# The spread of inverted sums as a planned step of its own, in a one-core attention and MLP kernel

## The chip, the core and the metric

The kernel runs on one core of a Trainium2 chip. Its engines are PE (matmul), ACT (activations, here above all exponentials), DVE (elementwise work), POOL and SyncE (SP), which here only issues DMAs. Each engine takes its instructions in order. The metric is the device time of one execution in microseconds (us), lower is better. Three runs of the kernel before took 878.48, 880.14 and 881.72 us; the median is 880.14.

## The reference

Softmax attention with 32 heads of 20 columns and an MLP with a mish activation are computed from the same input and blended by a sigmoid gate. Cut to what matters:

```python
x = A_x                                   # 1 x 2048 x 640, bf16
g = sigmoid((x * gate_w).sum(-1, keepdims=True))
qkv = (x @ wqkv) -> q, k, v of 32 heads x 2048 x 20
p = softmax(q @ k^T * 20 ** -0.5)
a = (p @ v, heads side by side) @ wo
h = x @ w1 + b1                           # w1: 640 x 1536
b = (h * tanh(log1p(exp(-|h|)) + max(h, 0))) @ w2
out = g * a + (1 - g) * b
```

## The kernel before

**Attention.** The scores are computed in units: one key tile of 128 rows against one chunk `c` of 512 queries, for one head. A group `(c, g)` is one chunk and four heads, 64 units; there are 32 groups and 2048 units. Three units make a slot of three PSUM banks, so there are 683 slots, and slot `s` is worked on at step `s`. PE writes the scores (`score_mms`, L1055), ACT takes the exponential of the whole slot in one instruction (`emit_e`, L1077) into one of five buffers, and PE multiplies by V (`pv`, L1180). Two slots of scores are in PSUM at a time, so PE writes those of step s + 2 while ACT works on s + 1. Each exponential can leave out its third unit, which DVE then computes with four instructions (`emit_x`, L1094, L1110 twice and L1112). Such an offloaded unit makes ACT's instruction 1024 columns wide instead of 1536. `choose` (L1118) decides at each step, from the reckoned backlog of DVE, whether one is taken. In the kernel before there are 202.

**The sums.** V carries a column of ones, so each group's accumulator (bank `ACC`) holds the sums of the exponentials. When a group is through, `group_done` (L1214) copies the accumulator to `OUNG` (L1258), and SyncE gathers the sums into `RR` (L1261). When the planner reckons these to be there, `invert` (L1264) has DVE take the reciprocal (L1265), has SyncE write it to DRAM (`SUMS`, L1266, 8 KB) and, right behind it, read it back spread over the partitions (`BCT`, L1268, 256 KB). L1268 waits for L1266 to land. `times` (L1225) is the multiplication on DVE (L1226) that waits for the spread. These steps come 31 times; the last group goes another way.

**The MLP and the rest.** Queries, keys, values and the MLP are background tasks: matmuls that PE does between the scores, into one PSUM bank (`FB`), which DVE evicts at the end of each task. `h_task` computes 256 rows by 256 columns of h (L845) and adds the bias on DVE (L855). It takes a block of w1 that `load_w1(n)` (L791, L801) has brought into one of two buffers, n mod 2. There are 48 loads of 320 KB: six blocks for each of eight row chunks. Load n + 2 is emitted when task n has emitted its last matmul, and waits for that matmul, because it overwrites the same buffer. From load `FIRST` = 12 on the buffers lie in other memory (in the trace under the name REG instead of W2R), and loads 12 and 13 wait for the tasks that used that memory before.

**The order.** Everything is written down by a planner that runs when the kernel is built. `Plan.add` appends an instruction to its engine's order and reckons its start and end from given costs: `cost` on the engine, `tail` until the result can be used, and for a DMA on SyncE `bulk`, the time for which it holds the queue. Instructions on an engine are executed in the order of these calls, and `Plan.finish` turns dependences into waits on semaphores. An instruction that waits holds back all that stand behind it on its engine, SyncE's DMA issues among them. The main loop (L1455) goes over the steps.

Work for DVE that need not be done at once waits in lists: `norm` (the work on the sums), `soon` (two lanes of offloaded units), `blend` (mish) and `bg`. `work(until)` (L400) takes from them, always the entry that could begin first, as long as it ends before `until` by the planner's clock. An entry is a cost, a function and a dependence; `safe` (L396) adds a margin to the dependence's reckoned end, 0.6 us for one on SyncE. Before each instruction that DVE must do at a fixed place, the helper `dve` (L390) lets `work` run up to the moment when that instruction could start, plus `SLACK` = 0.3 us, or plus `LATER` = 0.9 us when it evicts the background bank (`now["bank"]`) and the background work is not pressing (`now["rate"]` under 0.6). `fill_up` (L1439) adds matmuls without use where PE would be idle for too long: repeated scores, or products into the background bank (`spin`, L1433, which the trace shows at L1436).

Of the kernel before, what the change touches and what calls it, by code (L numbers as in the profile page):

```python
# [54 lines left out]
WIDE = 0.60  # L55
# [2 lines left out]
LANES = 2  # L58
TAKEN = 3.3
SLACK = 0.3  # L60
LATER = 0.9
FREE = 0.2
RISK = {"pe": 0.1, "act": 0.3, "dve": 0.5, "pool": 1.2, "sp": 0.6}
CHAIN = 3.0
# [151 lines left out]
def bass_gated_mix__softmax_full_mha__dense_activation_mish__prompt_kernel(  # L216
# [19 lines left out]
    def sb(name, shape, dt):  # L236
        return st.enter_context(nc.sbuf_tensor(name, shape, dt))
# [21 lines left out]
    RR = sb("RR", [P, 16], FP32)  # L259
# [12 lines left out]
    SUMS = nc.dram_tensor("SUMS", [HG, CW], FP32, kind="Internal")  # L272
# [31 lines left out]
    def w1b(n):  # L304
        return AREAS[n >= FIRST][0][:, n % 2, :, :]
# [6 lines left out]
    def otn(c, g, fast):  # L312

        return QT[:, g, (c - 2) * CW:(c - 1) * CW] if fast and c >= 2 else OTN[:, c % 2, g, :]
# [18 lines left out]
    def attention(pl, fast):  # L333
# [8 lines left out]
        norm = deque()  # L342
# [47 lines left out]
        def dve(fn, deps=(), cost=0.1, kind="F"):  # L390

            ready = max([pl.now["dve"], *(d.t1 + HOP for d in deps if d is not None)])
            work(ready + (LATER if fast and now["rate"] < BUSY and now["bank"] else SLACK))
            return pl.add("dve", fn, deps, cost=cost, kind=kind)
# [5 lines left out]
        def work(until):  # L400
            while True:
                best = None
                lined = sorted([lane for lane in (*soon, blend) if lane], key=lambda lane: lane[0][3])
                for rank, todo in enumerate((norm, *lined, bg)):
                    if todo:
                        cost, fn, dep = todo[0][:3]
                        op = dep() if dep else None
                        begin = pl.now["dve"]
                        if op:
                            begin = max(begin, op.t1 if op.eng == "dve" and not op.slot else safe(op))  # L410
                        if begin + cost <= until and (best is None or begin < best[0] - 0.01):
                            best = (begin, todo, fn)
                if best is None:
                    return
                best[1].popleft()
                best[2]()

        def flush(done):

            while not done():  # L420
                ready = [lane for lane in soon if lane]
                first = min(ready, key=lambda lane: (lane[0][2]().t1 if lane[0][2] else 0.0, lane[0][3]))
                first.popleft()[1]()
# [32 lines left out]
        if fast:  # L456
# [328 lines left out]
                return Task([mm(f) for f in range(NFT)], w * COL, finish, due,  # L785
                            lambda: [*sq_ops[n], m_one] if len(sq_ops.get(n, ())) == NFT else None)

            w1_load, w1_last = {}, {}
            w2_load = []

            def load_w1(n):  # L791

                k = n % 6
                if n < 2:
                    deps = []
                elif n in (FIRST, FIRST + 1):
                    assert len(sq_ops) >= 4
                    deps = list(wkv_read)
                else:
                    deps = [w1_last[n - 2]]  # L800
                w1_load[n] = pl.add("sp", lambda e: e.dma_start(  # L801
                    w1b(n), B_w1[:, k * HW:(k + 1) * HW].rearrange("(f p) c -> p f c", p=P)),
                    deps, f"w1{n % 2}", cost=0.75, tail=1.7, bulk=1.5)

            def load_w2():
                w2_load.append(pl.add("sp", lambda e: e.dma_start(
                    W2, B_w2.rearrange("(f p) c -> p f c", p=P)),
                    [*(ei_free[(0, b)] for b in range(3)), w1_last[FIRST - 2], w1_last[FIRST - 1], *u_free], "w2", cost=0.6, tail=1.7, bulk=9.0))
# [401 lines left out]
        oung_free, rr_read, bc_read = [None], [None], [None]  # L1210
        spread_last = []
        end_done = []

        def group_done(c, g, step, last):  # L1214


            end = c == NC - 1 and g >= NG - 1

            def reads():
                if fast:  # L1220
                    return [low_last[0]] if c >= 2 else [zeros, *turned, *(k_moved if g >= 6 else ())]
                assert c < 2 or g > 0 or len(otn_read[c % 2]) == 8
                return otn_read[c % 2]

            def times(src, deps):  # L1225
                oung_free[0] = bc_read[0] = otn_done[(c, g)] = pl.add("dve", lambda e: e.tensor_tensor(  # L1226
                    otn(c, g, fast), src, BC, ALU.mult), [*deps, *reads()], cost=WIDE)
                if g == NG - 1:
                    otn_read[c % 2] = []

            if end:
                while norm:
                    norm.popleft()[1]()
                if (c, g) == groups[-1]:
                    flush(lambda: not any(soon))
                for at, w in ([cut[(c, g)]] if fast else [(n * HW, HW) for n in range(2)]):
                    cols = slice(at, at + w)
                    src, bc, rr = PS[:, ACC, cols], BC[:, cols], RR[:, at // 32:(at + w) // 32]
                    cost = w * COL * 2.6 + 0.09
                    if (c, g) != groups[-1]:  # L1240
                        held = OUNG[:, cols]
                        last = acc_free[0] = pl.add(
                            "dve", lambda e, src=src: e.tensor_copy(held, src), [last, oung_free[0]], cost=cost)
                        src = held
                    a = pl.add("dve", lambda e, src=src, bc=bc: e.transpose(bc, src), [last, bc_read[0]], cost=cost)
                    a = pl.add("dve", lambda e, bc=bc, rr=rr, w=w: e.reciprocal(rr, bc[:, 0:w:32]), [a, rr_read[0]], cost=0.15)
                    a = pl.add("dve", lambda e, bc=bc, rr=rr, w=w: e.transpose(
                        bc.rearrange("p (a r) -> p a r", r=32), rr.unsqueeze(2).to_broadcast([P, w // 32, 32])),
                        [a], cost=cost)
                    to = otn(c, NG - 1, fast)[:, cols]  # L1250
                    end_done.append(pl.add("dve", lambda e, src=src, bc=bc, to=to: e.tensor_tensor(
                        to, src, bc, ALU.mult), [a, *reads()], cost=cost))
                oung_free[0] = bc_read[0] = rr_read[0] = otn_done[(c, g)] = end_done[-1]
                return
            while oung_free[0] == "busy":
                norm.popleft()[1]()
            src = OUNG[:, :]
            ev = dve(lambda e: e.tensor_copy(src, PS[:, ACC, :]), [last, oung_free[0]], WIDE)  # L1258
            oung_free[0] = "busy"
            acc_free[0] = ev  # L1260
            got = pl.add("sp", lambda e: e.dma_start(  # L1261
                RR[:, :], OUNG[0:P:32, :].rearrange("j (r a) -> j r a", a=16)), [ev, rr_read[0]], "nr0", cost=0.55, tail=1.4)

            def invert():  # L1264
                r = pl.add("dve", lambda e: e.reciprocal(RR[:, :], RR[:, :]), [got], cost=0.25)  # L1265
                rr_read[0] = pl.add("sp", lambda e: e.dma_start(  # L1266
                    SUMS.ap().rearrange("j (r a) -> (j r) a", a=16), RR[:, :]), [r, *spread_last], "nr1", cost=0.4, tail=1.7)
                spread_last[:] = [pl.add("sp", lambda e: e.dma_start(  # L1268
                    BC, SUMS.ap().unsqueeze(1).to_broadcast([HG, 32, CW])),
                    [rr_read[0], bc_read[0]], "nr2", cost=0.55, tail=4.7)]  # L1270
                spread = list(spread_last)
                norm.append((WIDE, lambda: times(src, spread), lambda: spread[-1]))
            norm.append((0.25, invert, lambda: got))


        if fast:
# [30 lines left out]
            tasks.extend(h_task(hc, k, H_AT + int(H_STEP * (6 * hc + k))) for hc in range(2) for k in range(6))  # L1307
            tasks.sort(key=lambda t: t.due)
            later(H_AT - 90, lambda: (load_w1(0), load_w1(1)))
            rest = []  # L1310

# [308 lines left out]

    fast = Plan("f_")
    flags, outs = attention(fast, True)
    fast.finish(sem)
    full = Plan("g_")
    maxima(full)
    attention(full, False)
    full.finish(sem)

# [48 lines left out]
```

## Time and profile before

| | us |
|---|---|
| median of three runs | 880.14 |
| lowest, highest | 878.48, 881.72 |
| the profiled execution | 881.69 |
| its span, first to last instruction | 879.9 |
| mean granted clock of PE | 0.993 |

The page gives for each engine the time in which it was busy and its share of the span. The chain of waits is followed back from the last instruction: at each step to what released it. A row of waits names who waited for whom, with the total in us, how often, and the longest. In a timeline the columns are start, length, engine, line, operation and output<-input, and in brackets the idle time before it with what ended it; neighbouring instructions of one group are merged, and xN counts them. Rows with the queue's name (SPq) are DMA issues, not transfers. Rows of groups end with busy time, mean ns of one, and idle time before it. Rows that begin A:B are windows: length, then busy time and count of PE, weight loads, DVE, ACT and POOL, then PE's granted clock, the mean busy share of the 16 DMA engines, and GB/s.

### The profile page before, as it was taken

The numbers are of one execution on the slowest core, as the hardware profiler recorded it, in microseconds if no ns is written. First come the engines' busy times: TensorE is split into PE (matmuls) and PEld (weight loads), VectorE is DVE, ScalarE is ACT, GpSimd is POOL, SyncE is SP. The second block draws the span as 40 slices with busy tenths as digits, with TensorE's granted clock in tenths as the row PEclk, the third lists the DMA queues.
The fourth block names the chain that finished last, engine by engine and source line by source line (L and its number), as shares of the span: only waits on it lengthen the run. The fifth ranks groups of instructions, "written<-read, shape, count | busy, mean of one in ns | idle before, by whom it ended". The sixth has DMA issues, their size and how long they took to land.

```text
span 879.9 us, 15312 instructions
## 1 busy us (share of the span) xinstructions
PE 744.8 (85%) x6249; PEld 259.3 (29%) x6291; DVE 818.7 (93%) x1421; ACT 858.4 (98%) x714; POOL 15.4 (2%) x29
## 2 busy tenths in 40 slices
PE   8888888888878888888888888898888788998885
PEld 3232232222322233223223233333333233332222
DVE  5899999999588998999999999999999799999996
ACT  6999999999999999999999999999999799999996
POOL 2000000000000000000000000000000000000000
PEclk9999999999999999999999999999999899999999
DMA  9112110011122110131121121111211212010001
GB/s 215 28 50 60 56 32 13 8 49 37 41 60 63 57 57 28 44 100 37 41 64 42 54 74 31 46 32 40 69 48 43 72 34 71 21 32 18 14 14 35
DMA packets 69870, 42.44 MB, mean 48 GB/s; under 512 B 20472, under 2 KB 65776, under 8 KB 69744
## 3 DMA queue, kind: packets, MB, share of 16 engines
q1 hardware_dynamic: 67424, 40.89, 16.5%
q8 instruction: 52, 0.85, 0.4%
q10 hardware_dynamic: 2256, 0.47, 0.3%
q0 software_dynamic: 112, 0.01, 0.1%
q14 instruction: 26, 0.21, 0.1%
HBM read 33.97 MB, written 5.23 MB: 45 GB/s over the span
## 4 chain that ended last, share of the span: by engine, by line
ACT 95%; PE 2%; DMA 1%; DVE 1%; issue 0%; ACTq 0%
ACT ETS L1077 93%; ACT REG L877 2%; DMA REG<-in_B_w_dram 1%; ACT W2R L877 1%; PE PS L1055 1%; PE PS L490 1%; PE PS L845 0%; DVE HB L936 0%; PE PS L1436 0%; PE PS L649 0%; PE PS L658 0%; PE PS L1180 0%; PE PS L769 0%; PE PS L930 0%; DVE HB L855 0%
## 5 line engine op out<-in xcount | busy, mean ns | idle before, releaser
L1077 ACT ACTIVATE ETS<-PS 128x1536 bf16<-128x1536 f32 (+1 forms) x683 | 837.9, 1479 | 6.2 <-PE PS L1055 6.1
L1055 PE MATMUL PS<-QT,KT 32*128 32x512 bf16 (+1 forms) x2267 | 281.7, 379 | 114.7 <-ACT ETS L1077 102.9
L1180 PE MATMUL PS<-ETS,V_all 128*21 128x512 bf16 (+1 forms) x1901 | 211.5, 380 | 0.3 <-ACT ETS L1077 0.3
L1055 PEld LDWEIGHTS PS<-QT,KT 32*128 32x128 bf16 x2267 | 69.3, 91 | 324.9 <-ACT ETS L1077 302.6
L1180 PEld LDWEIGHTS PS<-ETS,V_all 128*21 128x21 bf16 x1901 | 48.6, 89 | 93.4 <-issue 89.1
L906 PE MATMUL PS<-W2R,HB 128*128 128x320 bf16 x384 | 71.6, 302 | 0.9 <-DVE OUTT L936 0.6
L1110 DVE SCALAR_TENSOR_TENSOR EM<-EM 128x512 f32<-128x512 f32 x101 | 68.9, 682 | 0.1
L1110 DVE SCALAR_TENSOR_TENSOR ER<-ER 128x512 f32<-128x512 f32 x101 | 68.7, 680 | 0.0
L1094 DVE TENSOR_SCALAR XE<-PS 128x512 f32<-128x512 f32 x80 | 54.7, 686 | 8.3 <-PE PS L1055 7.2
L845 PE MATMUL PS<-XB,REG 128*128 128x256 bf16 x360 | 55.2, 279 | 3.7 <-DMA REG<-in_B_w_dram 3.4
L1094 DVE TENSOR_SCALAR REG<-PS 128x512 f32<-128x512 f32 x74 | 50.7, 686 | 2.2 <-PE PS L1055 1.8
L538 PE MATMUL PS<-XB,WOQ 128*128 128x512 bf16 x135 | 42.2, 384 | 2.7 <-issue 2.4
L906 PEld LDWEIGHTS PS<-W2R,HB 128*128 128x128 bf16 x384 | 30.0, 97 | 36.7 <-issue 24.4
L855 DVE TENSOR_TENSOR HB<-PS,B1F 128x512 bf16<-128x512 f32 x48 | 32.9, 685 | 6.0 <-PE PS L845 5.8
L845 PEld LDWEIGHTS PS<-XB,REG 128*128 128x128 bf16 x360 | 29.9, 98 | 28.7 <-issue 22.3
L1094 DVE TENSOR_SCALAR W2R<-PS 128x512 f32<-128x512 f32 x48 | 32.9, 686 | 3.1 <-PE PS L1055 2.4
L896 DVE SCALAR_TENSOR_TENSOR U<-U,HB 128x512 f32<-128x512 f32 x48 | 32.8, 683 | 0.0
L895 DVE SCALAR_TENSOR_TENSOR U<-U 128x512 f32<-128x512 f32 x48 | 32.7, 680 | 0.0
L550 DVE CAST QT<-PS 128x512 bf16<-128x512 f32 x31 | 21.3, 687 | 7.2 <-PE PS L538 6.8
L1110 DVE SCALAR_TENSOR_TENSOR ER<-XE 128x512 f32<-128x512 uint16 x40 | 27.4, 685 | 0.2
L1110 DVE SCALAR_TENSOR_TENSOR EM<-XE 128x512 f32<-128x512 uint16 x40 | 27.3, 683 | 0.2
L1112 DVE SCALAR_TENSOR_TENSOR XE<-ER,XE 128x512 int32<-128x512 f32 x40 | 27.4, 684 | 0.1
(115 smaller groups left out, 797.3 us busy)
## 6 DMA issues: line engine op xcount, KB each, us to landing
REG<-in_B_w_dram SPq DMA_DIRECT2D x36, 320.0 KB, 3.2
BCT<-SUMS SPq DMA_DIRECT2D x31, 256.0 KB
W2R<-in_B_w_dram SPq DMA_DIRECT2D x12, 320.0 KB, 3.2
KT<-KS SPq DMA_DIRECT2D x28, 128.0 KB
KS<-OTN SPq DMA_DIRECT2D x16, 128.0 KB, 1.8
W2R<-in_B_w_dram SPq DMA_DIRECT2D x1, 1920.0 KB, 9.4
out_dram<-OUTT SPq DMA_DIRECT2D x24, 80.0 KB, 1.6
REG<-in_A_wqkv_dram SPq DMA_DIRECT2D x2, 700.0 KB, 8.2
```

Of the source, the lines that this page charges most:

```text
L538: return lambda e, bank: e.matmul(PS[:, bank, :], pads[:, b, f, :], xt(c)[:, f, :], start=(f == 0), stop=(f == NFT - 1))
L845: return lambda e, bank: e.matmul(PS[:, bank, i * HW:(i + 1) * HW], w1b(n1)[:, f, i * P:(i + 1) * P], xt(c)[:, f, cols], start=(f == 0), s ...
L855: ev = dve(lambda e: e.tensor_tensor(hb, PS[:, bank, :].rearrange("p (i t) -> p i t", i=2), bias, ALU.add), [last, *b1f, *sq_read.values() ...
L895: piece(WIDE, lambda e: e.scalar_tensor_tensor(U2[:, :], U2[:, :], EVEN[0], U2[:, :], ALU.add, ALU.mult))
L896: piece(WIDE, lambda e, to=to: e.scalar_tensor_tensor(U2[:, :], U2[:, :], EVEN[1], to, ALU.add, ALU.mult))
L906: return lambda e, bank: e.matmul(PS[:, bank, 0:HALF], HB[:, hc % 2, f, t * P:(t + 1) * P], W2[:, f, half * HALF:(half + 1) * HALF], start ...
L1055: op = pl.add("pe", lambda e, i=i, g=real(g), tile=tile, j=j, cols=cols, c=c, of_q=of_q: e.matmul(scores(s)[:, i, cols], KT[32 * j:32 * j ...
L1077: e_op[s] = pl.add("act", lambda e: e.activation(ETS[:, s % NETS, 0:n, :], scores(s)[:, 0:n, :], AF.Exp, scale=SCALE, bias=LIFT if fast el ...
L1094: ev_op[s] = dve(lambda e: e.tensor_scalar(y, scores(s)[:, 2, :], SCALE * ULPS, BIAS, ALU.mult, ALU.add), [s_op[s], ei_free[b], *(wkv_read ...
L1110: piece(WIDE, lambda e, v=m if i else f, i=i: e.scalar_tensor_tensor(m, v, STEPS[i], v, ALU.add, ALU.mult), lambda i=i: () if i else [lane ...
L1112: piece(WIDE, lambda e: e.scalar_tensor_tensor(x, m, LAST_STEP, y, ALU.mult, ALU.add))
L1180: lasts[n] = pl.add("pe", lambda e, tile=tile, h=real(g) * HG + j, j=j, src=src[:, cols], of_q=of_q, count=count: e.matmul(PS[32 * j:32 * ...
```

## The change

`invert` no longer issues the spread. It puts an entry `spread` into `norm`, at no cost, whose dependence is the write of the inverted sums; the spread is emitted when `work` takes that entry, and only then does the multiplication enter the list. The reckoned tail of the write grows from 1.7 to 2.8 us. Each load of w1 also depends on the last load emitted for the same of the two buffers. `LATER` becomes 0.5. The number of offloaded units becomes 204, as a result of the planner's reckoning.

```diff
-LATER = 0.9
+LATER = 0.5
...
-            w1_load, w1_last = {}, {}
+            w1_load, w1_last, w1_newest = {}, {}, {}
...
                     deps = [w1_last[n - 2]]
+                deps = [*deps, w1_newest.get(n % 2)]
                 w1_load[n] = pl.add("sp", lambda e: e.dma_start(
                     w1b(n), B_w1[:, k * HW:(k + 1) * HW].rearrange("(f p) c -> p f c", p=P)),
                     deps, f"w1{n % 2}", cost=0.75, tail=1.7, bulk=1.5)
+                w1_newest[n % 2] = w1_load[n]
...
             def invert():
                 r = pl.add("dve", lambda e: e.reciprocal(RR[:, :], RR[:, :]), [got], cost=0.25)
                 rr_read[0] = pl.add("sp", lambda e: e.dma_start(
-                    SUMS.ap().rearrange("j (r a) -> (j r) a", a=16), RR[:, :]), [r, *spread_last], "nr1", cost=0.4, tail=1.7)
+                    SUMS.ap().rearrange("j (r a) -> (j r) a", a=16), RR[:, :]), [r, *spread_last], "nr1", cost=0.4, tail=2.8)
+                norm.append((0.0, spread, lambda: rr_read[0]))
+
+            def spread():
                 spread_last[:] = [pl.add("sp", lambda e: e.dma_start(
                     BC, SUMS.ap().unsqueeze(1).to_broadcast([HG, 32, CW])),
                     [rr_read[0], bc_read[0]], "nr2", cost=0.55, tail=4.7)]
-                spread = list(spread_last)
-                norm.append((WIDE, lambda: times(src, spread), lambda: spread[-1]))
+                wide = list(spread_last)
+                norm.append((WIDE, lambda: times(src, wide), lambda: wide[-1]))
             norm.append((0.25, invert, lambda: got))
```

## The prediction

> **What bounds the kernel now.** I read the page's busy shares and its chain first, then the waits of ACT, then the stretch of the chain that is not ACT, with the timelines of ACT, SyncE's queue and PE around it.
>
> ```profile
> PE 744.8 (85%) x6249; PEld 259.3 (29%) x6291; DVE 818.7 (93%) x1421; ACT 858.4 (98%) x714; POOL 15.4 (2%) x29
> ACT 95%; PE 2%; DMA 1%; DVE 1%; issue 0%; ACTq 0%
> ACT ETS L1077 <- PE PS L1055: 6.1, 5, 3.8
> ```
>
> ACT is busy for 858.4 of 879.9 us and is 95% of the chain that ended last: the 683 exponentials set the pace, and there are two ways to be faster, less for ACT to do or fewer holes in it. The third row, from the waits, says that the exponentials stood idle for 6.1 us in five places, waiting for scores, and that one place alone is 3.8. The chain shows where that is:
>
> ```profile
> 679.68 6.30 ACT ETS L1077 x5
> ...
> 686.49 7.22 DMA REG<-in_B_w_dram
> 693.71 0.05 issue
> 693.76 1.25 PE PS L845 x5
> ```
>
> ```profile
> 690.49 1.35 ACT L1077 ACTIVATE ETS<-PS 128x1024 bf16<-128x1024 f32 x1
> 695.59 1.45 ACT L1077 ACTIVATE ETS<-PS 128x1536 bf16<-128x1536 f32 x1 [3.76 <-PE PS L1055]
> 697.85 2.36 ACT L1077 ACTIVATE ETS<-PS 128x1536 bf16<-128x1536 f32 x2 [0.81 <-PE PS L1055]
> ```
>
> The chain leaves ACT at 685.98 (679.68 + 6.30) for a load of w1 that took 7.22 us. ACT's timeline has two holes there, 3.76 and 0.81 us. SyncE's queue and PE say why:
>
> ```profile
> 680.42 0.37 SPq L801 DMA_DIRECT2D REG<-in_B_w_dram  x1
> 682.71 0.34 SPq L1266 DMA_DIRECT2D SUMS<-RR  x1
> 685.92 0.53 SPq L1268 DMA_DIRECT2D BCT<-SUMS  x1
> 686.49 11.17 SPq L801 DMA_DIRECT2D REG<-in_B_w_dram  x3
> 684.42 0.50 PE L845 MATMUL PS<-XB,REG 128*128 128x256 bf16 x3
> 693.76 1.25 PE L845 MATMUL PS<-XB,REG 128*128 128x256 bf16 x5 [3.42 <-DMA REG<-in_B_w_dram]
> DMA to landing us min/median/max: 3.0/3.2/7.2
>   PEld PS L845: 4.1, 2
>   PE PS L845: 3.4, 1
> ```
>
> Load 39 of w1 may overwrite its buffer when the L845 matmuls that end at 684.92 (684.42 + 0.50) are done. But the spread (L1268) stands ahead of it in SyncE's order and waits for the write of the inverted sums (L1266, issued 682.71) to land. So the load is issued at 686.49, 1.6 us late, directly behind 256 KB of spread, and takes 7.2 where the median of the 48 loads is 3.2. PE, which runs in order, stood 3.42 us at L845, and the scores queued behind it. The last two rows say that no other of the 48 loads held a matmul; two held a weight load, this one and one by 0.4.
>
> **The change, part by part.**
>
> *The late load.* The spread becomes an entry of the list `norm`, which the planner emits when it reckons that the write has landed. In the built program of the changed kernel the spread stands 2 to 6 steps (a step is one exponential) behind the write, and in 12 of the 31 groups loads, stores or fetches lie between. For the group of the stall the new order is: write and load 41 at step 538, spread at 542; load 39 is emitted at step 530, eight steps ahead of any of them, and used at 536. Without the wait it would be issued near 684.9 and land 3.2 later, at 688.1, while PE's last work before the stall was issued at 689.95. What the hole costs, from the starts in ACT's rows: 690.49 to 695.59 and 695.59 to 697.85 are 5.10 and 2.26 us, for one exponential of 1024 and one of 1536 columns. Their undisturbed distances come from two unbroken runs:
>
> ```profile
> L1077 ACT ACTIVATE ETS<-PS 128x1024 bf16<-128x1024 f32 x5 | 4.7, 1067 | 0.0
> L1077 ACT ACTIVATE ETS<-PS 128x1536 bf16<-128x1536 f32 x9 | 12.2, 1532 | 0.0
> ```
>
> Records overlap, so the distance is the busy time less the last record, over one fewer: (4.7 - 1.067)/4 = 0.91 and (12.2 - 1.532)/8 = 1.33 us. The hole cost 5.10 + 2.26 - 0.91 - 1.33 = 5.12 us. Were the load merely issued in time and still slow, the least gain would be the 1.6 of waiting; the most is 5.12. I take 5.12: issued in time, the load has nothing in front of it and goes by the median.
>
> *Two more units.* A unit is one 128x512 score tile whose exponential DVE does in four instructions (L1094, L1110 twice, L1112); 202 become 204, and two of ACT's wide exponentials become narrow: 2 x (1.33 - 0.91) = 0.84 us off ACT. DVE gets eight instructions more:
>
> ```profile
> 674.16 0.68 DVE L1112 SCALAR_TENSOR_TENSOR REG<-EM,REG 128x512 int32<-128x512 f32 x1
> 674.76 0.68 DVE L897 SCALAR_TENSOR_TENSOR U<-REG,U 128x512 f32<-128x512 f32 x1
> ```
>
> At 0.60 us each (start to start) that is 4.8 us, under the 61.2 that DVE is idle (879.9 - 818.7). If that cover is gone where they fall, evictions come late and the whole 4.8 is the loss; the gain is 0.84. I take 0.84: counted by stretches of 50 steps, none has over three narrow exponentials more than it had.
>
> *A fixed order of w1 loads.* A load now also waits for the load two before it into the same buffer. All but loads 12 and 13 already wait for matmuls that wait for that load, so this adds nothing to them. Loads 12 and 13 have more than 50 steps until use. I take 0, and 0 for both bounds: a landing of 3.2, or of 7.2, is hidden in 50 steps of 0.91 us and more.
>
> *Spread later.* Its own cost is a later multiplication (L1226). In the new order the multiplication stands 4 to 8 steps behind the spread, 8 of them in the widest case (step 392 to 400), so 3.6 to 10.6 us by the distances above. What a spread needs:
>
> ```profile
> 658.13 0.53 SPq L1268 DMA_DIRECT2D BCT<-SUMS  x1
> 660.00:662.00 2.00, 1.00 0.25 96
> 662.00:664.00 2.00, 1.00 0.06 20
> 690.00:692.00 2.00, 1.00 0.92 174
> 692.98 0.69 DVE L1226 TENSOR_TENSOR QT<-OUNG,BCT 128x512 bf16<-128x512 f32 x1 [1.44 <-DMA BCT<-SUMS]
> ```
>
> Alone (issued 658.13) it keeps a quarter of the DMA engines busy and is through soon after 662, about 4 to 5 us; beside loads it took until 692.98, 7.1 after its issue, and DVE waited 1.44. SyncE does not wait for the planner's step: with nothing held ahead of it the spread goes out as soon as the write has landed, as before. So 0 in most groups, 1.44 at most in one whose spread has a load in front. I take 0 and keep 1.44 as the bound.
>
> *LATER 0.9 to 0.5.* Before DVE evicts the background bank it may now overrun by 0.5 us of filler rather than 0.9. The bank comes free up to 0.4 us earlier; DVE may idle 0.1 more, since a filler is 0.60. This and the changed matmul order (64 fill-in matmuls of L1436's kind in place of 37) bear on the other places where ACT waits for scores: 6.1 - 3.76 - 0.81 = 1.5 us in three. Between all of them gone and twice as many, -1.5 to +1.5, I take half gone, -0.8, for the reason that both edits give PE more room.
>
> **Sum.** The profiled execution took 881.69 us, 1.79 over its span of 879.9. 881.69 - 5.12 - 0.84 - 0.8 = 874.9 us. The three runs shown are 878.48, 880.14 and 881.72; the profiled one is at the upper end, and I take the difference for a varying length of the hole. With the hole gone the sum stands beside any of them: 0.6% under the median.
>
> **The rivals.**
>
> *Holes at new places.* The order of PE's work differs from step 23 on, and where the granted clock halves is not planned:
>
> ```profile
> 829.00:832.00 3.00, 2.79 (x12) 0.64 (x10) 2.97 (x5) 3.00 (x3) 0.00 (x0) 0.55 0.23 82
> 829.94 1.89 PE L1436 MATMUL PS<-KT 128*128 128x512 bf16 x4
> 823.37 1.04 PE L1436 MATMUL PS<-KT 128*128 128x512 bf16 x4
> ACT ETS L1077 <- PE PS L1055: 1.2, 2, 0.8
> ```
>
> At a clock of 0.55 four fill-ins took 1.89 us instead of 1.04, and ACT lost 0.4 (1.2, the waits from 698 on, less 0.81). Seven such places more than now and no other gain: 881.69 - 5.12 - 0.84 + 7 x 0.4 = 878.5. For it: PE is only 85% busy. Against: in the present order it is one place in 165 us. The Trainium skill (TensorE: Matmul & The Clock Gate, Part 1) says that the clock halves after an idle window of about 3.4 us which runs free of the program; by that, the place moves from run to run whatever the order, and part of the spread of the three runs would be this. The row at 829 agrees that it comes without a long stop of PE.
>
> *The hole stays, elsewhere.* The change would not do what it says if another load falls right behind a spread. Candidate: load 20, emitted at step 397 and used at 401, five steps behind the spread of step 392. At 7.2 instead of 3.2 it is 4 us later, and the four steps until its use are 3.6 to 5.3 us long. Price up to the old hole: 881.69 - 0.84 - 0.8 = 880.1. Against it: a load now issued 4.6 us behind a spread held no matmul.
>
> ```profile
> 723.80 0.53 SPq L1268 DMA_DIRECT2D BCT<-SUMS  x1
> 728.43 11.11 SPq L801 DMA_DIRECT2D REG<-in_B_w_dram  x4
> ```
>
> *Slower: spreads held in the queue.* In nine later groups (writes at steps 218 to 581) a load, fetch or store that waits for PE or DVE stands between write and spread. SyncE is in order, so the spread waits too; then the multiplication on DVE, behind it the evictions, behind them PE's bank and the scores. At 1.44 us each the nine make 13 us: 874.9 + 13 = 887.9. It decides from the fifth group on, where 5 x 1.44 = 7.2 exceeds the 6.8 won. For it: DVE is 93% busy and in order. Against: the multiplication stands 4 to 8 steps behind, and the present trace has a single wait of DVE for a spread, inside the hole.
>
> **How the numbers follow.** The forecast 0.72, own range 872.6 to 877.5 (the -1.5 and +1.5 of the small waits and about 1 between runs); holes at new places 0.15; the hole elsewhere 0.05; spreads held 0.08. Half a per cent, about what a measurement of this kernel tells from no change, is 4.4 us, so faster means under 875.7: about three quarters of the forecast's cases, 0.53. Within: the rest of it, 0.19, with 0.15 and 0.05, 0.39. Slower: 0.08. The range 872.6 to 880.2 leaves the slower rival out above and some of the forecast below.
>
> **What would show it.** ACT's largest wait for scores falls from 3.8 to under 1; no L845 matmul waits for a DMA; the longest landing of a w1 load that is used within ten steps is near 4 us; 205 narrow exponentials instead of 203; DVE busy about 5 us more; DVE waits for BCT near nothing. A w1 wait of over 2 us, or several waits of DVE for BCT followed by waits of ACT, would make the forecast wrong.

## The result, and the profile after

| | before | changed |
|---|---|---|
| median (runs, lowest to highest), us | 880.27 (6 runs, 878.48 to 881.72) | 876.56 (6 runs, 875.90 to 876.89) |
| profiled execution, its time and span, us | 881.69, 879.9 | 876.85, 874.5 |
| time outside the span, us | 1.79 | 2.35 |

The ratio of the changed kernel to the one before is 0.9958 (95% interval 0.9945 to 0.9971): 0.42% faster, and the interval ends clear of 1. The forecast was 874.9 with a range of 872.6 to 880.2. The time is in the range, 1.7 us above the forecast, and just inside the half per cent that was called no change, to which the prediction gave a chance of 0.39 against 0.53 for faster. The direction is right, the gain smaller than reckoned.

The page of the changed kernel, busy shares and chain, answers to the first rows of the prediction:

```profile
PE 746.5 (85%) x6225; PEld 258.6 (30%) x6268; DVE 825.5 (94%) x1429; ACT 857.6 (98%) x714; POOL 15.4 (2%) x29
ACT 91%; DVE 4%; DMA 2%; PE 2%; issue 0%; SPq 0%; ACTq 0%
```

ACT has 0.8 us less to do (858.4 to 857.6), DVE 6.8 more (818.7 to 825.5). The groups by shape say where ACT's part comes from: 205 narrow exponentials, as forecast, where there were 203.

```profile
L1079 ACT ACTIVATE ETS<-PS 128x1024 bf16<-128x1024 f32 x205 | 228.7, 1199 | 0.6 <-PE PS L1057 0.6
```

The waits (us in total, times, longest), and who waited for a load of w1:

```profile
ACT ETS L1079 <- PE PS L1057: 1.1, 2, 0.6
DVE OTN L1228 <- DMA BCT<-SUMS: 1.6, 1, 1.6
```

```profile
  PEld PS L847: 0.2, 1
DMA to landing us min/median/max: 3.0/3.2/6.3
```

ACT's waits for scores fell from 6.1 us in five places to 1.1 in two, the longest from 3.8 to 0.6. No matmul of L847 (L845 before) waits for a load; one weight load waits 0.2. A load that takes 6.3 us is still there (load 1, issued at 80.51 and used 95 exponentials later), but nobody waits for it; of the loads used within ten exponentials of their issue the longest took 4.5 (load 33). New is a wait of DVE for a spread, 1.6 us, and DVE's 4% of the chain. SyncE's queue around the old hole:

```profile
676.12 0.37 SPq L802 DMA_DIRECT2D REG<-in_B_w_dram  x1
...
682.02 0.48 SPq L802 DMA_DIRECT2D REG<-in_B_w_dram  x1
684.58 0.34 SPq L1268 DMA_DIRECT2D SUMS<-RR  x1
685.90 0.37 SPq L802 DMA_DIRECT2D REG<-in_B_w_dram  x1
686.82 0.54 SPq L1273 DMA_DIRECT2D BCT<-SUMS  x1
```

Load 39 is the one at 676.12 (it landed in 3.0 us), 8 us ahead of the write of the group's sums (684.58); the two later loads also pass the spread. Busy time of each engine (PE, PEld, DVE, ACT, POOL), granted clock, DMA share and GB/s in the old hole's stretch, first of the kernel before, then of the changed one:

```profile
686.00:698.00 12.00, 8.21 (x58) 3.15 (x59) 7.44 (x13) 7.43 (x7) 0.00 (x0) 0.78 0.34 77
```

```profile
686.00:698.00 12.00, 9.41 (x76) 3.41 (x74) 11.97 (x21) 12.00 (x11) 0.00 (x0) 1.00 0.16 49
```

ACT is busy for all of the 12 us where it was busy for 7.43, and the clock is not halved there.

The wait of DVE has its cause in the chain of the changed kernel (start, us, what):

```profile
278.41 4.73 DMA KS<-OTN
...
283.16 0.53 SPq L582
...
284.29 7.17 DMA BCT<-SUMS
...
291.48 0.69 DVE OTN L1228
```

The fetches of keys at L582 wait for the store of KS to land, and the spread of the group written at step 218 stands behind them in SyncE's queue. It is issued at 284.29 and lands at 291.46; DVE's multiplication (L1228) stood 1.6 us. This is the mechanism of the slower rival, in one place.

**An account in ACT's time.** Below, the holes of ACT are counted as the prediction counted the old one: the distance between the starts of two instructions of ACT, less the usual distance for that pair, summed where it is over 0.06 us. The kernel before: 13.4 us, of which 5.1 are the hole at load 39 and 8.3 the rest. The changed kernel: 9.2, with no hole there. So -5.1 from the hole, -0.8 from the units, +0.9 from the rest, and +0.56 outside the span. These add up to -4.4, against -4.84 between the two profiled executions (881.69 and 876.85); the 0.4 left is not accounted for.

### The profile page after: what moved, and what is told of

Read it like the earlier page. It is cut to its first block, busy times and chain, and to the rows that moved or that the text cites. A ratio compares the mean times of both kernels' runs of the same rounds, so it can differ in the third digit from the quotient of the medians.

```text
span 874.5 us, 15265 instructions
## 1 busy us (share of the span) xinstructions
PE 746.5 (85%) x6225; PEld 258.6 (30%) x6268; DVE 825.5 (94%) x1429; ACT 857.6 (98%) x714; POOL 15.4 (2%) x29
## 4 chain that ended last, share of the span: by engine, by line
ACT 91%; DVE 4%; DMA 2%; PE 2%; issue 0%; SPq 0%; ACTq 0%
ACT ETS L1079 89%; ACT REG L879 2%; DMA BCT<-SUMS 1%; DMA OTN<-in_A_x_dram 1%; DMA KS<-OTN 1%; DVE EM L1112 0%; ACT W2R L879 0%; PE PS L1057 0%; DVE ER L1112 0%; DVE W2R L1114 0%; DVE XE L1096 0%; PE PS L847 0%; DVE HB L938 0%; DVE HB L857 0%; PE PS L1182 0%
## 5 line engine op out<-in xcount | busy, mean ns | idle before, releaser
L1057 PE MATMUL PS<-QT,KT 32*128 32x512 bf16 (+1 forms) x2217 | 276.5, 376 | 108.7 <-ACT ETS L1079 94.1
L847 PE MATMUL PS<-XB,REG 128*128 128x256 bf16 x360 | 55.4, 275 | 0.4
L847 PEld LDWEIGHTS PS<-XB,REG 128*128 128x128 bf16 x360 | 29.2, 97 | 26.6 <-issue 24.4
L1114 DVE SCALAR_TENSOR_TENSOR XE<-EM,XE 128x512 int32<-128x512 f32 x40 | 27.2, 680 | 0.0
```

The source lines that it names most:

```text
L847: return lambda e, bank: e.matmul(PS[:, bank, i * HW:(i + 1) * HW], w1b(n1)[:, f, i * P:(i + 1) * P], xt(c)[:, f, cols], start=(f == 0), s ...
L1057: op = pl.add("pe", lambda e, i=i, g=real(g), tile=tile, j=j, cols=cols, c=c, of_q=of_q: e.matmul(scores(s)[:, i, cols], KT[32 * j:32 * j ...
L1114: piece(WIDE, lambda e: e.scalar_tensor_tensor(x, m, LAST_STEP, y, ALU.mult, ALU.add))
```

## The experiments

In the diffs, lines are cut to what differs. The kernel before ran beside them, at medians of 879.46 us (25 runs) and 879.47 (15 runs) in two sessions; ratios are taken within a session.

### One spread moved in the kernel before

The finished list of the kernel before is kept, but for one entry: the spread that stood ahead of load 39 goes behind it.

```diff
     flags, outs = attention(fast, True)
+    loads = [op for op in fast.ops if op.slot in ("w10", "w11")]
+    at39 = fast.ops.index(loads[39])
+    held = [i for i, op in enumerate(fast.ops[:at39]) if op.slot == "nr2"][-1]
+    fast.ops.insert(at39, fast.ops.pop(held))
```

> The kernel before, with one DMA moved: the spread that stands ahead of load 39 of w1 in SyncE's order (step 536) stands behind that load. Nothing is planned anew; every other engine's order is the kernel's before. Theory: the hole of 5.1 us at 690 to 698 us is the whole of what the change removes, made by the load waiting 1.6 us behind the spread and then sharing the DMA engines with it. Then load 39 lands about 3.2 us after an issue near 685, no L845 matmul waits for a DMA, and the time falls by about 5 us: ratio 0.9942, near 875.2 us, below the changed kernel. Rival: the gain comes from the new plan as a whole, and taking the load out only passes the stall on to load 40 or to the multiplication by the spread: ratio 0.998 or more.

Measured: 876.73 us (876.18 to 878.09), ratio 0.9967 (0.9956 to 0.9978). SyncE's queue and the waits of this kernel:

```profile
685.05 0.37 SPq L801 DMA_DIRECT2D REG<-in_B_w_dram  x1
685.63 0.53 SPq L1268 DMA_DIRECT2D BCT<-SUMS  x1
```

```profile
ACT ETS L1077 <- PE PS L1055: 1.1, 2, 0.6
```

Load 39 goes out at 685.05 instead of 686.49, lands in 3.1 us instead of 7.2, and the hole is gone: ACT's waits for scores are the changed kernel's 1.1 to the digit. One entry of the queue brings 0.33% where the whole change brought 0.42%; the two ratios' intervals overlap, and the 0.09% between them, 0.8 us, is the size of the two units that this kernel lacks. The expected size was missed: 0.9942 was reckoned from a hole of 5.1 us, and this gain is 2.9 (further down, the hole is 3.3 to 3.4 in other executions). The rival's 0.998 or more did not come.

### The wait kept, the sharing removed

The hole had two causes, the wait (1.6 us late) and the sharing with the spread (7.2 instead of 3.2). The same move, but load 39 still waits for the write.

```diff
+    loads[39].deps.append([op for op in fast.ops[:held] if op.slot == "nr1"][-1])
+    fast.ops.insert(at39, fast.ops.pop(held))
```

> The kernel before with load 39 ahead of the spread, as in the run with one spread moved, but load 39 still waits for the write of the inverted sums to land. It takes the hole's two parts apart: the wait in the queue is kept, the sharing of the DMA engines with the spread is gone. Theory: the wait costs nothing by itself, since a load issued near 686 lands 3.2 us later at 689.2 and PE comes to it at 690.3; the hole is all sharing. Then no L845 matmul waits for a DMA and the ratio is that of the run with one spread moved, 0.9967 within 0.001. Rival: the 1.6 us of waiting is a part of the hole: PE waits 1 us or more there, ratio 0.998 or more.

Measured: 877.10 us (876.73 to 878.78), ratio 0.9975 (0.9965 to 0.9986). SyncE's queue and ACT:

```profile
685.98 0.37 SPq L801 DMA_DIRECT2D REG<-in_B_w_dram  x1
686.71 0.54 SPq L1268 DMA_DIRECT2D BCT<-SUMS  x1
```

```profile
697.55 1.45 ACT L1077 ACTIVATE ETS<-PS 128x1536 bf16<-128x1536 f32 x1 [0.17 <-PE PS L1055]
699.87 2.79 ACT L1077 ACTIVATE ETS<-PS 128x1536 bf16<-128x1536 f32 x2 [0.87 <-PE PS L1055]
```

The load is as late as before (685.98), lands in 3.1, and no matmul waits for it. The small hole that is left (0.17 and 0.87) comes 12 us later, behind a spread that is now 0.8 us later (DVE waited 1.2 for it); the profile is of the slowest of the eight executions. The ratio is within 0.001 of 0.9967, as the theory expected, but its interval reaches into what the rival expected, so the load's rows decide. At the old time of issue, but without the spread in front, it holds nobody: with the sharing gone, the wait costs no hole there. No run kept the sharing and took the wait away.

### The spread as four transfers

If the sharing is the cause, it can be cured with no entry moved. Each spread is issued as four transfers of 32 partitions; the order stays the kernel before's. (The diff leaves out the counting of the four landings.)

```diff
-    BC, SUMS.ap().unsqueeze(1).to_broadcast([HG, 32, CW])),
+    BCT[32 * j:32 * j + 32, :], SUMS.ap()[j:j + 1, :].to_broadcast([32, CW])) for j in range(HG)],
```

> The kernel before with each spread issued as four DMAs of 32 partitions, one for each head, in place of one whose outermost dimension is 4; no order differs. In the kernel before a lone spread keeps a quarter of the DMA engines busy for some 4 us. Theory: that is the outermost dimension of 4 (so the Trainium skill, DMA: Bandwidth & Descriptors, on how many engines a DMA uses); four DMAs of 32 rows use all 16 engines, a lone spread is through in 2 us or less at a DMA share over 0.5, and load 39, though issued some 1.6 us later still, lands in about 4.5 us instead of 7.2; the hole shrinks by about 1 us, ratio 0.997 to 1.000. Rival: the bytes set the pace: the lone spread keeps its length, and the hole grows by the three further issues of 0.5 us each, ratio over 1.001.

Measured: 876.85 us (876.55 to 877.97), ratio 0.9973 (0.9962 to 0.9983), at the good edge of what was expected. SyncE's queue, and the stretch of a spread that runs alone (columns as above), first of the kernel before, then of this one:

```profile
685.57 1.72 SPq L1270 DMA_DIRECT2D BCT<-SUMS  x4
687.33 5.62 SPq L803 DMA_DIRECT2D REG<-in_B_w_dram  x3
```

```profile
660.00:662.00 2.00, 1.66 (x16) 0.80 (x16) 1.97 (x5) 2.00 (x3) 0.00 (x0) 1.00 0.25 96
```

```profile
659.00:660.00 1.00, 0.57 (x6) 0.10 (x3) 1.00 (x3) 1.00 (x2) 0.00 (x0) 1.00 0.33 113
660.00:661.00 1.00, 0.91 (x8) 0.54 (x9) 1.00 (x3) 1.00 (x3) 0.00 (x0) 1.00 0.46 121
```

Load 39 goes out at 687.33, later than in the kernel before (686.49) and still behind a whole spread, yet it lands in 3.2 us where 4.5 was expected. PE stands 0.44 us for it instead of 3.42, and ACT's hole falls to 0.5 by starts, with no wait for scores there (1.5 in all). The one transfer keeps 0.25 of the DMA engines busy, which is 4 of 16 if those are busy throughout, until soon after 662; the four reach 0.46, less than the 0.5 that was expected, and nothing is left of them after 661.

Two more loads say the same. Loads 15 and 29 of the kernel before also stand 0.57 us behind a spread and land in 6.2 and 5.8 us; they hold nobody, because they are used 13 and 16 exponentials after their issue. Behind the four transfers (0.47 us) all three of these loads land in 3.1 to 3.2. So a spread that is confined to a quarter of the engines is what delays a load right behind it, not its 256 KB. The Trainium skill (DMA: Bandwidth & Descriptors, "Why a DMA increments its semaphore by 16 and not by 1") says that the number of engines follows from the outermost dimension of the access pattern. Here that is HG = 4, and the trace's 0.25 agrees.

### The changed kernel with the spread as four transfers

> The changed kernel with the same four DMAs for each spread. Theory: a spread is then never late: DVE's wait of 1.6 us for BCT at 291 us goes or shrinks below 0.5, and nothing else waits, since SyncE has room for 1.6 us more in each of 31 groups; ratio 0.995 to 0.9965 to the kernel before. Rival: the further issues delay loads of w1 behind them, and an L847 matmul waits for a DMA: 0.998 or more.

Measured: 875.57 us (875.08 to 875.73), ratio 0.9956 (0.9943 to 0.9970). DVE waits for no spread, and ACT's waits for scores are 1.1 in two places again. Its median is the lowest of all versions run here, but its ratio is within 0.0002 of the changed kernel's, so nothing shows it to be faster than that.

### The change's other parts

The spread as a step of its own, and with it the 204 units, without LATER's change and without the fixed order of loads:

```diff
+                norm.append((0.0, spread, lambda: rr_read[0]))
+            def spread():
```

> The changed kernel with LATER = 0.9 and without the fixed order of loads: only the spread as a step of its own and the tail of 2.8. It has 204 units, too, but 45 fill-in matmuls where the changed kernel has 64. Theory: the step holds the whole gain: no load of w1 used within ten steps lies directly behind a spread, no matmul waits for a DMA, ratio 0.994 to 0.997. Rival (LATER makes the gain): 0.999 or more.

Measured: 880.01 us (878.88 to 882.36), ratio 1.0005 (0.9995 to 1.0015). The expectation fell. No matmul waited for a load, but ACT has new holes at another place (its timeline, then the chain):

```profile
518.53 2.79 ACT L1077 ACTIVATE ETS<-PS 128x1536 bf16<-128x1536 f32 x2 [1.03 <-PE PS L1180]
522.14 4.63 ACT L1077 ACTIVATE ETS<-PS 128x1024 bf16<-128x1024 f32 x4 [0.81 <-PE PS L1180]
```

```profile
513.94 1.25 PE PS L1055 x15
...
516.61 0.92 PE PS L906 x6
...
517.95 0.56 PE PS L1180 x4
```

ACT waits for a buffer ETS that the multiplications with V (L1180) have still to read. The waits there are 1.84 us. The chain from 513.94 to 518.53 is PE alone, without a pause: fifteen score matmuls where a slot has three, and the MLP's L906, stand ahead of the L1180 that ACT waits for. So L1180 came late in PE's order, and no wait for DVE is on that path; why the plan has it so was not tested. Besides, the clock was halved from 114 to 117 us (granted 0.50), with a hole of 0.8 at 116.

LATER at 0.5 alone in the kernel before (200 units):

```diff
-LATER = 0.9
+LATER = 0.5
```

> The kernel before with LATER = 0.5 and nothing else. It has 200 units. The new plan puts another load right behind a spread: load 33, emitted at step 496 just behind a write and its spread, used at step 501. Theory: the hole comes back there, by the same mechanism: load 33 is issued behind the spread, takes 6 to 7 us to land, an L845 matmul waits 1 to 4 us for it, and ACT loses 2 to 5 us; with 0.84 us for two units fewer the time is within 2 us of the kernel before, ratio 0.998 to 1.003. Rival (LATER makes the gain): 0.997 or less, and no matmul waits for a DMA.

Measured: 881.47 us (878.99 to 883.18), ratio 1.0016 (1.0002 to 1.0030). As expected, another load fell behind a spread (SyncE's queue, then the waits):

```profile
632.85 0.53 SPq L1268 DMA_DIRECT2D BCT<-SUMS  x1
633.43 2.71 SPq L801 DMA_DIRECT2D REG<-in_B_w_dram  x2
```

```profile
ACT ETS L1077 <- PE PS L1055: 4.1, 8, 1.5
```

Load 33, issued at 633.43, took 5.9 us, a matmul of L845 stood 1.5, and ACT lost 1.8, a little less than the 2 to 5 expected. The hole moved instead of going away. So neither part is faster alone: the spread as a step of its own opens a hole at 518, LATER alone one at load 33. The changed kernel, with both and the fixed order of loads, has an order with neither hole; nothing here shows that to be more than chance.

The fixed order of loads alone:

```diff
+                deps = [*deps, w1_newest.get(n % 2)]
+                w1_newest[n % 2] = w1_load[n]
```

> The kernel before with the fixed order of w1 loads alone; two loads, 12 and 13, get a wait they had not, nothing else moves. Theory: no effect, 878 to 883 us, the hole at load 39 as in the kernel before (2 to 5.2 us). Rival: the waits of loads 12 and 13 hold what stands behind them in SyncE's queue, and a matmul or a fetch there waits that did not: over 0.5 us more of holes in the stretch of loads 12 and 13.

Measured, one execution: 880.83 us (the kernel before beside it 880.79). Its holes are those of the kernel before, with 3.3 us at load 39. In the holes the part does nothing, as forecast. Outside the span lie 2.13 us, against 1.79 in the kernel before beside it; more on that below.

### The held spread of step 218

In the changed kernel, the spread that made DVE wait is put directly behind its write.

> The changed kernel with one DMA moved: the spread of the group whose sums are written at step 218 stands directly behind its write again, ahead of the load and the two fetches of keys (which wait for a store of keys to land) that stand between them in the changed kernel. No other order differs. Theory: that spread went out late because it was held in the queue, so DVE waited 1.6 us for it at 291 us and ACT lost about 0.9 us between there and 330 us. Then DVE's wait for BCT goes, the shortfalls of ACT at 284 to 330 us shrink by about 0.9 us, and the ratio is about 0.001 below the changed kernel's 0.9958. Rival: DVE's wait was hidden: no change of ACT's shortfalls there.

Measured: 876.33 us (875.69 to 877.36), ratio 0.9960 (0.9945 to 0.9974). DVE's wait is gone, and ACT's holes between 284 and 330 us are 0.8 where the changed kernel had 1.4; but the time can't be told from the changed kernel's. Nor is the fall shown to come from the move: the second execution of the changed kernel itself (below) has 0.8 there too, with DVE still waiting 1.0. That the wait was hidden from ACT, as the rival has it, stays possible. The profiled execution also lost 0.9 to a halved clock in a place where the order of both kernels is the same. First the changed kernel, then this one:

```profile
171.00:174.00 3.00, 2.88 (x24) 0.81 (x23) 2.69 (x7) 3.00 (x3) 0.00 (x0) 1.00 0.03 3
```

```profile
171.00:174.00 3.00, 3.00 (x19) 0.52 (x12) 2.29 (x6) 2.61 (x2) 0.00 (x0) 0.50 0.03 3
```

### The slower rival, made to happen

In the changed kernel, spreads are put as late in SyncE's order as three steps ahead of their multiplication; 15 of the 31 move.

```diff
+    for held in [op for op in fast.ops if op.slot == "nr2"]:
+        ...
+        to = max([k for k in range(i, users[0]) if fast.ops[k].eng == "sp" and fast.ops[k].step <= use - 3])
+        fast.ops.insert(to, fast.ops.pop(i))
```

> The changed kernel with its spreads put as late in SyncE's order as three steps before their multiplication: 15 of the 31 move behind one or more loads, stores or fetches that wait for PE or DVE. The orders of all other engines are the changed kernel's. It tries the slower rival of the forecast and its price. By the rival: each held spread makes DVE wait 1 to 3 us for BCT, the evictions behind it come late, and ACT loses as much: 15 places, 10 us or more, ratio 1.005 or more. By the forecast's own theory a wait of DVE is partly hidden from ACT: DVE waits for BCT in 5 to 15 places, 10 to 25 us in total, and the time grows by less than half of that, ratio 0.998 to 1.006. If spreads were covered whatever their place: DVE waits under 3 us in all, ratio 0.997 or less.

Measured: 933.61 us (932.31 to 934.79), ratio 1.0618 (1.0602 to 1.0634), far above the 0.998 to 1.006 of the forecast's own theory. The slower rival's open-ended 1.005 or more holds, with a price per place above its 1 to 3 us. The waits, and one place from SyncE's queue to DVE, PE and ACT:

```profile
ACT ETS L1081 <- PE PS L1059: 53.1, 46, 5.0
DVE OTN L1230 <- DMA BCT<-SUMS: 23.6, 8, 5.0
DVE QT L1230 <- DMA BCT<-SUMS: 21.9, 8, 4.9
```

```profile
268.75 0.34 SPq L1270 DMA_DIRECT2D SUMS<-RR  x1
273.55 0.33 SPq L570 DMA_DIRECT2D KS<-OTN  x1
275.26 1.10 SPq L584 DMA_DIRECT2D KT<-KS  x2
276.40 0.51 SPq L1275 DMA_DIRECT2D BCT<-SUMS  x1
...
283.45 0.69 DVE L1230 TENSOR_TENSOR OTN<-OUNG,BCT 128x512 bf16<-128x512 f32 x1 [4.53 <-DMA BCT<-SUMS]
...
286.22 1.22 PE L849 MATMUL PS<-XB,W2R 128*128 128x256 bf16 x5 [3.65 <-DVE OTN L600]
...
288.03 1.02 ACT L1081 ACTIVATE ETS<-PS 128x1024 bf16<-128x1024 f32 x1 [3.55 <-PE PS L1059]
290.29 2.10 ACT L1081 ACTIVATE ETS<-PS 128x1024 bf16<-128x1024 f32 x2 [1.23 <-PE PS L1059]
```

The spread stands 7.65 us behind its write, behind a store and two fetches. DVE stands 4.53, then PE 3.65 for an eviction behind it (L600), then ACT 3.55 and 1.23. The mechanism is as the prediction described it, and it costs more than its own wait: DVE waited 45.5 us (23.6 + 21.9), the kernel lost 57 (933.61 - 876.56; by the two ratios 58), and the granted clock fell to 0.952 from 0.997. How much of the 57 belongs to the clock was not taken apart.

### The two kernels again

One more execution of the changed kernel and two of the one before, unchanged, ask how much of the account above belongs to the order and how much to the execution.

> The kernel before, unchanged, profiled in another execution. Theory: the hole at load 39 has a varying length. The first profiled execution, 881.69 us, lay at the upper end and had a hole of 5.12; the medians (880.27 before, 876.56 after) put the usual one nearer 3. So this execution's time less its hole should be 876 to 877.5, whatever the time is: at 879.5 the hole is 2 to 3.5. Rival: the hole is the same 5.1 in every execution, and the scatter of the times comes from pieces of halved clock at places that vary (0.4 to 0.9 us each); then the hole is within 0.3 of 5.1, and the difference shows as fewer or more such pieces.

> The kernel before once more. Theory: time less hole is 876 to 877.5 again, and load 39 is issued within 0.3 us of 1.6 late while its landing varies. Rival: hole of 5.1 again, load 39 lands in 7.2 again within 0.3.

> The changed kernel, unchanged, profiled in another execution. Theory: the small holes belong to the order that was built: DVE waits 1.3 to 1.8 us for the spread of the group at step 218 again, ACT loses about 1.4 between 284 and 330, and its holes add up to 8.5 to 10. Rival: they vary from execution to execution, and the 9.2 of the first profile against 8.3 of the kernel before is chance; then the sum differs from 9.2 by more than 1, or the wait at step 218 is under 0.8.

ACT at the hole of the kernel before, in the second of these:

```profile
690.12 1.35 ACT L1077 ACTIVATE ETS<-PS 128x1024 bf16<-128x1024 f32 x1
693.58 1.45 ACT L1077 ACTIVATE ETS<-PS 128x1536 bf16<-128x1536 f32 x1 [2.11 <-PE PS L1055]
695.64 1.45 ACT L1077 ACTIVATE ETS<-PS 128x1536 bf16<-128x1536 f32 x1 [0.61 <-PE PS L1055]
```

By starts the hole is 3.46 + 2.06 - 0.91 - 1.33 = 3.3 us. All holes of ACT in each execution, sorted the same way (a halved clock is read from the windows; "base" is the time less the two columns before it):

| execution | time, us | hole at load 39 | holes at a halved clock elsewhere | base | all other holes | outside span |
|---|---|---|---|---|---|---|
| before, first | 881.69 | 5.1 | 0.7 | 875.9 | 7.6 | 1.8 |
| before, second | 882.03 | 3.4 | 2.3 | 876.3 | 7.7 | 1.8 |
| before, third | 878.73 | 3.3 | 0 | 875.4 | 8.4 | 1.8 |
| fixed order alone | 880.83 | 3.3 | 0.8 | 876.7 | 7.8 | 2.1 |
| changed, first | 876.85 | 0 | 0 | 876.9 | 9.2 | 2.4 |
| changed, second | 875.86 | 0 | 0 | 875.9 | 8.0 | 2.1 |

Both theories were half right. The hole does vary, from 3.3 to 5.1 us, and so does load 39's landing (7.2, 6.0 and 6.2 us). The clock has a part in it, too: at the hole it was halved for 6.8 us in the first execution and for 3.4 in each of the other two, by windows of 1 us. But the time less the hole was not 876 to 877.5: it is 878.6 in the second execution and 875.4 in the third. The longest time has a hole of 3.4; pieces of halved clock at other places, 2.3 us, make up most of the rest. The small holes of the changed kernel, 9.2, were 8.0 the second time, a difference of over 1, as the rival said; ACT's holes between 284 and 330 us were 0.8 instead of 1.4. The wait of DVE at step 218 was there again, 1.0 instead of 1.6, under the 1.3 to 1.8 expected.

## Why the prediction was right, and where its sum was off

**The late load: right, in its cause and its size.** Moving that one spread gives 0.33% of the change's 0.42%, and four of the rows named beforehand came: ACT's longest wait under 1 (0.6), no matmul waiting for a load, 205 narrow exponentials, a longest landing near 4 (4.5) for a load used within ten steps. Of the others, DVE is 6.8 us busier instead of about 5, and it waits 1.6 us for BCT instead of near nothing. The term of 5.12 was the size of that execution; the profiles pair up as -5.1. In the other three profiles with this hole it is 3.3 to 3.4. With that size the terms give 3.3 + 0.84 - 0.5 (outside the span, below) = 3.6, which fits the 3.7 between the medians, where the forecast lies 5.4 under the median before. The prediction also took "issued in time" and "nothing in front of it" as one; the run with the wait kept and the one with four transfers show that the second was most of it.

**Two more units: as far as ACT goes right.** ACT's busy time fell by 0.8. DVE's busy time grew by 6.8, more than the 4.8 reckoned for their eight instructions; a cost of that shows in no wait of its own in the profile.

**LATER and the matmul order: the step that failed.** "I take half gone, -0.8" rested on 1.5 us of ACT's waits in three places, with room on PE as its only reason. Those places are 0.5 at 10 us, 0.6 at 245 and 0.4 at 832. The first two are in the changed kernel as they were, 0.5 and 0.6. The third was a piece of halved clock, and the third execution of the kernel before does not have it either. So the term is nothing in its own rows. In all small holes that carry no halved clock, 7.6 to 8.4 us before and 8.0 to 9.2 after, no gain shows. And LATER alone puts another load behind a spread.

**Outside the span: a term that was missing.** The sum took 1.79 as fixed; the changed kernel has 2.35 and 2.06 in its two profiles, the kernel before 1.79 to 1.83 in three. The other executions bear this out, to 0.1 us: 2.3 to 2.6 in the changed kernel's six runs, 1.8 to 2.0 in 40 of the kernel before. It goes with the fixed order of w1 loads, a term that the prediction took as 0: the other versions that have it lie at 2.1 to 2.5, those without it at 1.8 to 2.0. But the changed kernel with four transfers has it too and lies at 1.9, so the cause is open. With 0 for the small holes and 0.5 for this, the sum is 881.69 - 5.12 - 0.84 + 0.5 = 876.2, against 876.85 in the profiled run and 876.56 as the median. The forecast's own range does not follow from its terms either: -1.5 and +1.5 for the small waits and 1 between runs give 873.2 to 878.2, not 872.6 to 877.5; the measured time lies in both.

**The varying length of the hole,** by which the prediction explained the spread of the runs before, is only a part of it. The hole varies by 1.8 us, but between the longest and the shortest of the three profiles, 3.3 us apart (882.03 and 878.73), it differs by 0.1; halved clock elsewhere makes 2.3, and the rest is open.

**The rivals.** Holes at new places: a piece of halved clock cost ACT 0.7 to 1.5 us by starts in the profiles of the kernel before, more than the 0.4 reckoned from waits. But the two profiles of the changed kernel have none that cost ACT anything, where that rival wanted seven. The prediction took its row at 829 as agreeing with the rule that it cites; that row has a halved clock with no stop of PE over 0.62 us just ahead of it, which an idle window does not cover (see the last section). The hole elsewhere: not in the changed kernel, where load 20 was issued 6.8 us behind its spread, landed in 3.0 and held no matmul. With one part of the change alone it did come, at load 33. Spreads held: real, once, 1.0 to 1.6 us of DVE's time. Of the nine places that the rival counted, eight made DVE wait for nothing; a multiplication 4 to 8 steps behind its spread was cover enough there. Its price per place depends on how late the spread is: where it was forced late, 57 us for 16 waits is 3.6 us each and not 1.44, and nine such would have cost 32 us, not 13; the one that came by itself cost ACT 0.6 us (1.4 - 0.8), if that difference is its doing at all.

## What to carry to other kernels

When one engine is busy for 98% of the span, read the few holes of that engine one by one: a single entry of an in-order queue, here a wait with 256 KB behind it in front of a load that was needed next, was worth 0.33% by itself (0.22 to 0.44), and moving it by hand gave what the whole change gave, as far as the runs can tell. Ask of a transfer how many DMA engines it uses: splitting the broadcast in four took away all but 0.5 us of the same hole with no entry moved. Run the parts of a change alone: here two of them gained nothing by themselves, and each brought a hole of its own. And profile the kernel before more than once before a hole's length is put in a sum: the same hole was 5.1, 3.4 and 3.3 us.

## What the runs showed of the hardware that was not expected

**The clock halves in one execution and not in another, on the same work.** The kernel before, around 414 us, first and second execution:

```profile
413.00:414.00 1.00, 0.39 (x3) 0.10 (x3) 1.00 (x4) 1.00 (x2) 0.00 (x0) 1.00 0.00 0
414.00:415.00 1.00, 0.78 (x8) 0.31 (x9) 1.00 (x3) 1.00 (x3) 0.00 (x0) 1.00 0.09 8
```

```profile
413.00:414.00 1.00, 0.39 (x3) 0.10 (x3) 1.00 (x4) 1.00 (x2) 0.00 (x0) 1.00 0.00 0
414.00:415.00 1.00, 0.77 (x7) 0.21 (x7) 1.00 (x3) 1.00 (x3) 0.00 (x0) 0.62 0.08 7
```

PE's timeline there, first and second execution, with its longest stop since 406:

```profile
414.22 0.39 PE L1055 MATMUL PS<-QT,KT 32*128 32x512 bf16 x3 [0.53 <-ACT ETS L1077]
```

```profile
414.23 0.61 PE L1055 MATMUL PS<-QT,KT 32*128 32x512 bf16 x3 [0.53 <-ACT ETS L1077]
```

Up to there the starts of PE's groups agree in the two within 0.01 us. Then the second execution runs at half clock until 417.7, and ACT loses 0.86 us. The Trainium skill (TensorE: Matmul & The Clock Gate, Part 1) has the halving after an idle window of about 3.4 us that runs free of the program. That it falls differently on the same work agrees; that the window must be idle does not, as PE's longest stop here is 0.53 us.

**What goes behind a spread varies.** Load 39 directly behind the spread landed in 7.2, 6.0 and 6.2 us in three executions of the same program, loads 15 and 29 behind theirs in 5.6 to 6.2. Load 39 landed in 3.0 to 3.3 wherever no spread stood right in front of it or the spread was split.
